# A planned attention + squared-ReLU kernel: P.V shares a ring of four PSUM banks with the layers, x of batch 1 is turned by DMA, landings are planned later

## The chip, the cores and the metric

One core of one Trainium2 chip. The metric is the device time of one execution in microseconds. Before the change three runs gave 374.03, 371.48 and 372.93 us, median 372.93 us.

## The reference

Attention with a T5 relative-position bias, followed by a feed-forward block without bias, all in fp32:

```python
# q, k, v: (8 batches, 8 heads, 576 positions, 64), bias_table: (32 buckets, 8 heads)
scores = q @ k^T / 8 + bias[bucket(|i - j|), head]      # distances >= 128 share the last bucket
attn   = exp(scores - max); attn /= sum + 1e-9
x      = (attn @ v) with heads side by side             # (4608 tokens, 512)
h      = maximum(x @ w_in, 0)                           # w_in (512, 2048)
out    = (h * h) @ w_out                                # w_out (2048, 512), out fp32
```

## The kernel before

**Attention.** The 64 (batch, head) problems are taken as 32 *pairs* of heads, four pairs to a batch (`pair(p)`). q and k of a pair arrive as fp16 in a staging buffer (`stg`, five of them) by a casting DMA of POOL's queue, and have to be turned so that the 64 head dimensions lie on partitions. In batches 0 and 1 TensorE turns them (L662) and DVE or ScalarE copies them out of PSUM; from batch 2 on (`DT_QK`) SP's queue turns them with a DMA transpose (L645). The scores are computed transposed: four runs of 128 keys by 512 queries (L707, two 64-row halves of the array, one per head), plus the last 64 keys (`last_keys`, L758) and the last 64 queries (`last_queries`, L733), which read copies spread by L689 into block-diagonal tiles `qz`. ScalarE takes the exponential of each from PSUM (L720, L768, L743), with no maximum subtracted; the far bucket's bias is taken off the table, so only a band round the diagonal has to be multiplied by `tb_sb`, the exponential of the table, on DVE (L801). Then P.V (L837 for the last keys, L844 for the rest) gives 128 queries by two heads with a column of sums, in two parts per pair (three and two query tiles). DVE takes the reciprocal of the sums (L861) and multiplies (L866) into a tile `x`.

**x turned.** Layer 1 wants x with its 512 features on partitions (`xt`, a window of three batches). For batches below `DT_X` (0 and 1) TensorE transposes 128x128 blocks into PSUM (`x_turn`, L904; four transposes for each of five query tiles) and DVE (L626) or ScalarE (L624) copies them to `xt`. From `DT_X` on SP's queue does it with a DMA transpose for each part (L882).

**Layers.** Tokens go in nine groups of 512. Layer 1 of a group is 16 tiles of four matmuls with 512 columns (L1257), ReLU on ScalarE (L1286), square on DVE (L1296). Layer 2 is done with seven products in place of eight (`second`, L1028), on sums that DVE makes of the squares (L983) and of w_out (L958); each product is 2x8 matmuls of 256 columns, and its banks are read into `y` by ScalarE (L1062) or DVE (L1056). Part of layer 1 of the last two groups is done the same way (`by_sevens`, L1182). Results leave on SP's queue (L1084).

**PSUM.** Eight banks: two double banks `st` for scores, one bank `pv` for P.V (ring `r_pv`), three banks `f` (ring `r_g`) for the turns, the layers and the tables.

**The order of the work.** [...] each engine and each queue runs its own list of instructions in order, and waits at each for the semaphores of what it needs. The lists come from a planner (`Plan`). Every piece of work is an `Op` with engines and an assumed duration, what it depends on, the buffers it holds, and a due time; `schedule()` plays a clock forward, and on each engine takes the piece that can start first, and of several the one due first. A DMA is two pieces: its issue on the queue's engine, and its flight on a resource `DMA`, which takes packets/16 ns in turn; those who need the data start after that and a latency (`LAT`). In the plan before, landings are cheap (a `DMA` duration and 1800 ns), so the consumers of a DMA stand soon behind it in their engine's list. The order that results is written down: it holds whether or not the chip is as fast as the plan assumed. Due times are formulas (`T = nominal(p)`, `G0 + GP * g`).

Of the kernel before, what the change touches and what calls it, by code (L numbers as in the profile page):

```python
# [10 lines left out]
FP32 = mybir.dt.float32  # L11
# [22 lines left out]
DT_X = 2  # L34
RELU_DVE = 0
NSTG, NQK, NPT, NV, NX, NGB, NRT, NY, NF = 5, 4, 3, 3, 6, 2, 4, 4, 2
QUIET, LATER = 5000.0, 9000
# [25 lines left out]


# [17 lines left out]
class Op:  # L82
    __slots__ = (
        "engs", "fn", "deps", "bufs", "due", "after", "mode",
        "users", "wait", "ready", "eng", "start", "end", "seq",
    )

    def __init__(self, engs, fn, deps, bufs, due, after, mode):
        self.engs, self.fn, self.bufs, self.due = engs, fn, bufs, due
        self.after, self.mode = after, mode  # L90
        self.deps = [d for d in deps if d is not None]
        self.users, self.ready = [], after
        self.start = self.end = self.eng = None
# [3 lines left out]
LAT = {"PE": 200.0, "ACT": 90.0, "DVE": 90.0, "POOL": 120.0, "DMA": 1800.0, "SP": 0.0, "XB": 2000.0}  # L97
SWITCH = 105.0


class Plan:
# [3 lines left out]
    def add(self, engs, fn, deps=(), bufs=(), due=0.0, after=0.0, mode=None):  # L105
# [3 lines left out]
        for b in op.bufs:  # L109
            b.left += 1  # L110
        return op

    def schedule(self):
# [12 lines left out]
        while len(done) < len(self.ops):  # L126
            best = None
            for e in engines:
                pick = None
                for op in waiting[e]:  # L130
# [3 lines left out]
                    key = (max(at, now[e]), op.due if op.due > -1e8 else op.ready - 1e9, op.seq)  # L134
# [15 lines left out]
            now[e] = op.end  # L150
# [9 lines left out]
            for u in op.users:  # L160
                u.wait -= 1
                if not u.wait:
                    u.ready = max(
                        [u.after]
                        + [d.end + (LAT[d.eng] if tuple(u.engs) != (d.eng,) else 0.0) for d in u.deps]
# [32 lines left out]
def kernel(  # L198
# [64 lines left out]
    pv_ps = [psum.tile([128, 512], FP32, name=f"pv{i}") for i in range(1)]  # L263
    g_ps = [psum.tile([128, 512], FP32, name=f"f{i}") for i in range(3)]

    P = Plan()
    r_set, r_pv, r_g, r_lane = Ring(2), Ring(1), Ring(3), Ring(8)
# [6 lines left out]

    def loader(eng_name, eng, out_, in_, packets, deps=(), bufs=(), due=0.0, after=0.0, turn=-1e9):
# [3 lines left out]
            {eng_name: 720.0 if eng_name == "POOL" else 600.0},  # L279
# [6 lines left out]
        return P.add({"DMA": packets / 16}, None, [issue], list(bufs) + lane, due if lane else turn), issue  # L286
# [9 lines left out]
    def load(*args, **kw):  # L296
# [8 lines left out]
            const(t[0, 0:2].rearrange("h (p j) d -> p h (j d)", j=6)), 192 * (150, 20)[w], (), [b_stg[0]], due=-5,  # L305
# [3 lines left out]
    l_id = load("SP", nc.sync, const(idsel_sb), const(id_d.ap()), 128 * 27, due=-1)  # L309
# [3 lines left out]
        128 * 27, due=0,  # L313
    )
    l_far = load("ACT", nc.scalar, const(far_sb), const(bias_table[NBK - 1 : NBK, :]), 27, due=1)
    l_oh = load("SP", nc.sync, const(oh_sb), const(oh_d.ap()), 128 * 60, due=4)
# [15 lines left out]
    z_one = P.add({"DVE": 60.0}, lambda: io(nc.vector.memset(one_sb, 1.0)), due=-2)  # L332
# [15 lines left out]
        {"DVE": 100.0},  # L348
# [8 lines left out]
    for c in range(6):  # L357
# [11 lines left out]
        o = P.add({"PE": 16 * 55.0}, t_mm, [o_eb, l_oh], [t_b], LEAD + TAB, 0.0, "f")  # L369
# [27 lines left out]
    def fill(ap, value, ns, due, after, deps=()):  # L397
        return P.add({"DVE": ns}, lambda: io(nc.vector.memset(ap, value)), deps, (), due, after)

    zz = z_sb.bitcast(FP32)  # L400
    z_fix = [[fill(zz[:, 0], 0.0, 150.0, 10, QUIET)], [fill(zz[:, 1:], 0.0, 300.0, 11, LATER)]]
    first = [
        fill(pt_sb[:, :, PW:], 1.0, 150.0, 20, LATER),
        fill(pm_sb[:, :, S:], 1.0, 150.0, 20, LATER),
# [4 lines left out]
            fill(va_sb[:, a, :, :, 64:66], VSC, 150.0, 30, at),  # L409
            *(fill(vm_sb[ds(64 * e, 64), a, :, e, 64:66], VSC, 90.0, 30, at, [o]) for e in range(2)),  # L410
        ]
        for a, ns, at in ((slice(0, 1), 250.0, QUIET), (slice(1, NV), 500.0, LATER))
# [3 lines left out]
        fill(stg[i][w][96:128, 512:640].bitcast(FP32), 0.0, 90.0, 40 + i, 25000.0)  # L416
# [25 lines left out]
    def load_six(p, w):  # L442
# [8 lines left out]
                192 * 75, (), [b_stg[p]], pdue(),  # L451
# [3 lines left out]
    def load_rows(p, w):  # L455
# [8 lines left out]
                512 * 34.5, s_fix, [b_stg[p]], pdue(),  # L464
            )
            for e in range(2)
# [5 lines left out]
                128 * 34.5, s_fix, [b_stg[p]], pdue(),  # L472
# [14 lines left out]
    def load_v_head(b, h):  # L487
# [4 lines left out]
            512 * 34.5, v_fix[min(b, 1)], [b_v[b]], pdue(),  # L492
# [3 lines left out]
    def load_v_tail(b):  # L496
        for e in range(2):
# [4 lines left out]
                256 * 34.5, v_fix[min(b, 1)], [b_v[b]], pdue(),  # L502
# [857 lines left out]
```

The softmax here doesn't subtract the row's maximum and nothing guards it: scores larger than these inputs give would overflow.

## Time and profile before

| what | value |
|---|---|
| three runs | 371.48, 372.93, 374.03 us (median 372.93) |
| the profiled execution: first to last instruction (its span, the only time it has) | 369.4 us |
| median less span | 3.5 us, outside the first and last instruction |
| TensorE (PE) busy | 353.9 us, 96% |
| DVE, ScalarE (ACT), GpSimd (POOL) busy | 277.0, 262.5, 185.4 us |
| granted TensorE clock | 1.000 |
| DMA moved | 44.26 MB in 162293 packets |

How to read it: the span is 369.4 us of the one execution that the profiler recorded. An engine is busy while it has an instruction in flight; matmuls overlap in TensorE's pipeline, so their own durations are longer than their distance. A row of a timeline gives start, length, engine, line, operation, output<-inputs, number of instructions, and in brackets the idle time before it with what ended it. DMA-issuing instructions of POOL are shown as busy on POOL; those of SP's queue are named SPq.

### The profile page before, as it was taken

The page shows a single profiled execution, that of the slowest core. Times are in us where ns is not written, and L with a number is a line of the kernel's source. Part 1 is how long each engine was busy: PE and PEld are TensorE (multiplying, and loading weights), DVE is VectorE, ACT ScalarE, POOL GpSimd, SP SyncE. Part 2 cuts the span into 40 slices and gives each one's busy share as a digit, 9 for nine tenths or more (in the row PEclk, how much of TensorE's full clock was granted, in tenths as well). Part 3 has the DMA queues.
Part 4 walks back from the last instruction along what each step waited for, and adds up shares of the span by engine and source line. Part 5 has one row for each costly group of instructions (what it writes and reads, how often), then busy time and mean ns, then how long its engine had stood idle before and what let it go on. Part 6 is the DMA issues. An engine that isn't in the chain of part 4 may idle for free.

```text
span 369.4 us, 10030 instructions
## 1 busy us (share of the span) xinstructions
PE 353.9 (96%) x3966; PEld 246.0 (67%) x3966; DVE 277.0 (75%) x618; ACT 262.5 (71%) x377; POOL 185.4 (50%) x343
## 2 busy tenths in 40 slices
PE   3978999899999999999999999999999999999996
PEld 2656455556587457877785468745876689657885
DVE  3997789957785498658965687669755987888693
ACT  4998989688575887689766887688758880586420
POOL 8897359295655676757845556777614100000000
PEclk9999999999999999999999999999999999999999
DMA  9999999795999999998999999999985112200022
GB/s 171 156 135 172 187 175 93 96 112 94 175 113 146 165 128 140 132 167 150 125 130 149 114 161 108 157 169 141 108 124 130 46 36 63 88 2 28 30 86 87
DMA packets 162293, 44.26 MB, mean 120 GB/s; under 512 B 145734, under 2 KB 162246, under 8 KB 162246
## 3 DMA queue, kind: packets, MB, share of 16 engines
q0 software_dynamic: 74208, 14.53, 52.0%
q1 hardware_dynamic: 87696, 28.80, 42.2%
q8 instruction: 31, 0.51, 0.6%
q10 hardware_dynamic: 342, 0.30, 0.3%
q14 instruction: 16, 0.13, 0.1%
HBM read 36.88 MB, written 9.44 MB: 125 GB/s over the span
## 4 chain that ended last, share of the span: by engine, by line
PE 88%; DVE 7%; ACT 2%; DMA 1%; issue 1%; ACTq 0%; DVEq 0%
PE f L1257 32%; PE f L1028 29%; PE pv L844 9%; PE st L707 8%; PE pv L837 2%; DVE pt L801 2%; PE st L758 2%; PE st L733 2%; PE st L1182 1%; DVE x L866 1%; DMA g<-in_q_dram 1%; PE f L662 1%; PE f L363 1%; ACT pm L768 1%; PE pv L1182 1%; DVE s L983 1%
## 5 line engine op out<-in xcount | busy, mean ns | idle before, releaser
L720 ACT ACTIVATE pt<-st 128x1024 f16<-128x1024 f32 x128 | 127.4, 1026 | 30.8 <-PE st L707 30.8
L1257 PE MATMUL f<-xt,w_in_sb 128*128 128x512 f16 (+4 forms) x656 | 127.8, 338 | 0.2 <-ACT xt L624 0.2
L1286 ACT ACTIVATE rt<-f 128x512 f16<-128x512 f32 x132 | 77.8, 602 | 38.4 <-PE f L1257 35.3
L1257 PEld LDWEIGHTS <-w_in_sb 128*128 128x128 f16 x656 | 57.9, 98 | 52.1 <-issue 12.2
L1296 DVE TENSOR_TENSOR g<-rt 128x512 f16<-128x512 f16 x132 | 57.6, 441 | 20.8 <-ACT rt L1286 19.8
L801 DVE TENSOR_TENSOR pt<-pt,tb_sb 128x1536 f16<-128x1536 f16 (+2 forms) x96 | 60.7, 640 | 15.6 <-ACT pt L720 15.1
L1028 PEld LDWEIGHTS <-g 128*128 128x128 f16 x576 | 54.5, 98 | 13.0 <-issue 4.7
L280 POOL DMA_DIRECT2D qs<-in_q_dram x79 | 55.4, 716 | 4.4 <-DMA w_out_sb<-in_moe_w_out_dram 2.6
L280 POOL DMA_DIRECT2D ks<-in_k_dram x79 | 55.3, 702 | 0.7 <-issue 0.6
L844 PE MATMUL pv<-va,pt 128*128 128x65 f16 x1280 | 54.7, 193 | 0.0
L844 PEld LDWEIGHTS <-pt 128*128 128x128 f16 x1280 | 50.2, 97 | 3.2 <-issue 1.4
L1056 DVE SCALAR_TENSOR_TENSOR y<-f,y 128x512 f32<-128x512 f32 (+1 forms) x47 | 31.4, 667 | 23.8 <-PE f L1028 23.6
L1028 PEld LDWEIGHTS <-s 128*128 128x128 f16 x432 | 41.2, 98 | 9.0 <-issue 2.5
L707 PE MATMUL st<-qt,kt 64*128 64x512 f16 x256 | 40.3, 385 | 0.9 <-ACT pt L743 0.4
L689 POOL COPY qz<-kt 64x64 f16<-64x64 f16 x58 | 18.5, 319 | 44.4 <-DMA kt<-ks 34.7
L689 POOL COPY qz<-qt 64x64 f16<-64x64 f16 x61 | 18.9, 310 | 35.4 <-DMA qt<-qs 27.3
L837 PE MATMUL pv<-vm,pm 128*128 128x130 f16 x160 | 35.3, 221 | 1.2 <-DVE x L866 1.0
L1028 PE MATMUL f<-w_out_sb,s 128*128 128x256 f16 x288 | 36.1, 273 | 0.0
L1028 PE MATMUL f<-wt,g 128*128 128x256 f16 x288 | 35.7, 273 | 0.0
L1028 PE MATMUL f<-w_out_sb,g 128*128 128x256 f16 x272 | 34.5, 273 | 0.7 <-ACT y L1062 0.7
L866 DVE TENSOR_TENSOR x<-pv,r 128x384 f16<-128x384 f32 x64 | 31.4, 490 | 2.0
L983 DVE TENSOR_TENSOR s<-g,s 128x1024 f16<-128x1024 f16 x36 | 25.6, 711 | 0.4
(90 smaller groups left out, 338.7 us busy)
## 6 DMA issues: line engine op xcount, KB each, us to landing
out_dram<-y SPq DMA_DIRECT2D x34, 256.0 KB, 2.4
f<-in_v_dram SPq DMA_DIRECT2D x24, 256.0 KB, 4.3
qs<-in_q_dram POOLq DMA_DIRECT2D x48, 64.0 KB, 4.4
ks<-in_k_dram POOLq DMA_DIRECT2D x48, 64.0 KB, 3.5
w_in_sb<-in_moe_w_in_dram POOLq DMA_DIRECT2D x4, 512.0 KB, 7.2
w_out_sb<-in_moe_w_out_dram POOLq DMA_DIRECT2D x4, 512.0 KB, 10.6
qs<-in_q_dram POOLq DMA_DIRECT2D x7, 144.0 KB, 4.6
ks<-in_k_dram POOLq DMA_DIRECT2D x7, 144.0 KB, 5.5
```

The source lines that it names most:

```text
L280: lambda: io(eng.dma_start(out=out_(), in_=in_())),
L689: io(eng.tensor_copy(out=dst[qb.slot][rw, rw], in_=src[qb.slot][rw, 512:576]))
L707: nc.tensor.matmul(sets_ps[st.slot][:, e, :], kt[rw, ts(jt, 128)], qt[rw, 0:512], start=True, stop=True,)
L720: nc.scalar.activation(out=p5(pts[pb.slot])[:, jt, :, 0:512], in_=sets_ps[st.slot], func=EXPF, scale=SCALE)
L801: io(nc.vector.tensor_tensor(out=a, in0=a, in1=t, op=MULT))
L837: nc.tensor.matmul(ps[:, i, :, :], pm[:, c : c + 128], vm[:, hp, :, 0:65], start=True, stop=False)
L844: nc.tensor.matmul(ps[:, i, e, :], pt[:, (2 * jt + e) * S + c : (2 * jt + e) * S + c + 128], va[:, jt, 2 * hp + e, 0:65], start=False, sto ...
L866: nc.vector.tensor_tensor(out=xs[xb.slot][:, qt0 : qt0 + nq, :].rearrange("p t (e d) -> p t e d", e=2), in0=ps[:, :, :, 0:64], in1=rs[rb.s ...
L1028: nc.tensor.matmul(home[bf.slot][:, ts(s_, HALF)], left(c, s_), right(c), start=(c == 0 and (s_ == 0 or apart) and (own or i not in before ...
L1257: nc.tensor.matmul(g_ps[bank.slot][:, a:z], w_in_sb[:, kk, ts(nt, 128)], xt_sb[:, kk, c : c + z - a], start=(kk == 0), stop=(kk == 3),)
L1286: io(nc.scalar.activation(out=rts[rb.slot], in_=g_ps[bank.slot], func=RELUF))
L1296: nc.vector.tensor_tensor(out=gs[gb1.slot][:, nt, :], in0=rts[rb.slot], in1=rts[rb.slot], op=MULT)
```

## The change

- `DT_X` goes from 2 to 1: x of batch 1 is turned by eight DMA transposes of SP's queue (L882) in place of 20 TensorE transposes (L904) and five copies.
- `pv_ps` and `g_ps` are one list of four banks, and `r_pv` is `r_g`: P.V, the turns, the tables and the layers take turns in one ring.
- The planner's figures: durations of issues, memsets and others; a landing has `SPARE` added to its DMA duration, 300 ns for the first loads and 2000 ns from batch 2 on and for DMA transposes and outputs; `over()` lets an engine's next piece start before the last has ended by the plan's clock; `AGAIN` sets what one engine waits between two of its own dependent pieces.
- `DUES`: a table that replaces the due times of some 200 pieces (by number) with others, so that the lists of all engines come out in another order.
- Memsets of constant parts may start from 1000 ns in place of 5000 and 9000, and those of the staging rows (`s_fix`) may run on POOL too (`fill_late`).
- `f1_last` keeps all layer-1 pieces of a group, not the last one made: who overwrites `xt` waits for all of them.

```diff
-DT_X = 2
+DT_X = 1
-QUIET, LATER = 5000.0, 9000
+QUIET, LATER = 1000.0, 1000.0
+DUES = """
+2:-11720 4:-7240 8:-7990 18:-18030 24:-23230 33:38700 40:-11430 56:-6380 58:-12660 60:-28280 62:-24060 64:-12660
...
+2155:-48680 2318:434840 2337:-29070
+"""
-LAT = {"PE": 200.0, "ACT": 90.0, "DVE": 90.0, "POOL": 120.0, "DMA": 1800.0, "SP": 0.0, "XB": 2000.0}
+LAT = {"PE": 200.0, "ACT": 90.0, "DVE": 90.0, "POOL": 120.0, "DMA": 1700.0, "SP": 0.0, "XB": 2000.0}
+SPARE = 300.0, 2000.0
+AGAIN = {"ACT": 30.0, "DVE": 30.0}
+def over(e, took, op):
+    if op.fn is None:
+        return op.spare
+    if e == "ACT":
+        return 123.0 if took > 400 else 60.0
+    if e == "DVE":
+        return 85.0 if took >= 240 else -10.0
+    return 40.0 if e == "POOL" else 0.0
...
+    def land(self, packets, deps, bufs, spare):
+        op = self.add({"DMA": packets[0] * packets[1] / 16 + spare}, None, deps, bufs, -1e9)
+        op.spare, op.packets = spare, packets
         return op
...
-            now[e] = op.end
+            now[e] = op.end - (over(e, took, op))
...
-    pv_ps = [psum.tile([128, 512], FP32, name=f"pv{i}") for i in range(1)]
-    g_ps = [psum.tile([128, 512], FP32, name=f"f{i}") for i in range(3)]
+    g_ps = pv_ps = [psum.tile([128, 512], FP32, name=f"f{i}") for i in range(4)]
-    r_set, r_pv, r_g, r_lane = Ring(2), Ring(1), Ring(3), Ring(8)
+    r_set, r_g, r_lane = Ring(2), Ring(4), Ring(8)
+    r_pv = r_g
...
-            {eng_name: 720.0 if eng_name == "POOL" else 600.0},
+            {eng_name: (775.0 if packets[0] >= 512 else 665.0) if eng_name == "POOL" else 500.0},
...
-        fill(stg[i][w][96:128, 512:640].bitcast(FP32), 0.0, 90.0, 40 + i, 25000.0)
+        fill_late(stg[i][w][96:128, 512:640].bitcast(FP32), 110.0, 1e5, 30000.0)
...
-                evac.append(P.add({"DMA": 1160.0}, None, [o], [qb, b_stg[p]], -1e9))
+                evac.append(P.land((640, 23.0), [o], [qb, b_stg[p]], SPARE[1]))
...
-                t = x_last[hp, part] = P.add({"DMA": 232.0 * nq}, None, [t], [xb], -1e9)
+                t = x_last[hp, part] = P.land((128 * nq, 23.0), [t], [xb], SPARE[1])
...
-        return [f1_last[old // GT]] if old >= 0 else []
+        return f1_last[old // GT] if old >= 0 else []
...
+    for x in DUES.split():
+        i, due = x.split(":")
+        P.ops[int(i)].due = float(due)
     for op in P.schedule():
```

## The prediction

> **What bounds the kernel now.** I read the page's busy shares and slices first:
>
> ```profile
> span 369.4 us, 10030 instructions
> PE 353.9 (96%) x3966; PEld 246.0 (67%) x3966; DVE 277.0 (75%) x618; ACT 262.5 (71%) x377; POOL 185.4 (50%) x343
> PE   3978999899999999999999999999999999999996
> ACT  4998989688575887689766887688758880586420
> ```
>
> TensorE is idle only in the first eight slices (74 us) and the last. Busy is not work, though. In the timeline two successive layer-2 matmuls start 0.109 us apart and layer-1 matmuls 0.216 us apart; from 75 us on nearly every start stands at that distance, plus about 0.095 us where the array goes over to 64-row score tiles or back. So behind 75 us the time is TensorE's work, and only what adds or removes matmuls, or lets TensorE run dry, can move it. What it waits for:
>
> ```profile
> PE f L662 <- ACT qs L481: 5.9, 1, 5.9
> PE f L904 <- DVE x L866: 1.3, 3, 0.6
> PE st L758 <- ACT pt L720: 1.3, 2, 0.8
> PE pv L837 <- DVE x L866: 1.0, 3, 0.5
> PE f L1028 <- ACT y L1062: 0.7, 1, 0.7
> ```
>
> 5.9 us is the start: q lands, is cast, is turned. The rest falls in two places, seen in the windows (each engine's busy time):
>
> ```profile
> core 0: us, PE busy (x) PEld busy (x) DVE busy (x) ACT busy (x) POOL busy (x), PEclk, DMA share, GB/s
> 0.00:38.80 38.80, 28.27 (x542) 20.10 (x542) 29.02 (x87) 31.58 (x44) 32.97 (x65) 1.00 1.29 160
> 38.80:62.00 23.20, 23.19 (x248) 12.26 (x247) 20.24 (x49) 21.34 (x32) 12.70 (x22) 1.00 1.31 160
> 62.00:75.00 13.00, 11.30 (x139) 7.75 (x136) 11.58 (x29) 9.14 (x13) 6.27 (x13) 1.00 0.75 84
> ```
>
> First the *ramp*: up to 38.8 us, where layer 1 begins, TensorE has little to do and ScalarE's exponentials set the pace (31.6 of the 33.8 us since its cast at 5.0). Then the *boundary* of batch 1, where layer 2 of group 0 begins and x of batch 1 is turned:
>
> ```profile
> 62.94 1.92 PE L1028 MATMUL f<-w_out_sb,g 128*128 128x256 f16 x16
> 65.55 1.91 PE L1028 MATMUL f<-w_out_sb,g 128*128 128x256 f16 x16 [0.69 <-ACT y L1062]
> 68.82 0.34 PE L904 MATMUL f<-id_sb,x 128*128 128x128 f16 x3
> 69.61 0.68 PE L904 MATMUL f<-id_sb,x 128*128 128x128 f16 x9 [0.45 <-DVE x L866]
> 70.97 0.33 PE L904 MATMUL f<-id_sb,x 128*128 128x128 f16 x3
> 71.62 0.45 PE L904 MATMUL f<-id_sb,x 128*128 128x128 f16 x5 [0.32 <-DVE x L866]
> 72.54 1.02 PE L1257 MATMUL f<-xt,w_in_sb 128*128 128x512 f16 x4 [0.24 <-ACT xt L624]
> ```
>
> Count in starts: 16 matmuls from 62.94 should end at 64.69, the next starts at 65.55 (0.86 late). A transpose takes 0.058 us (nine from 69.61 to 70.13), so 69.61 is 0.62 late and 71.62 is 0.48; the four matmuls at 71.91 need 0.22, so 72.54 is 0.41 late. Together 2.4 us.
>
> [...] 96% busy hides the distances above, which I use instead. [...] v loads of SP's queue issued between 20 and 45 us, beside the weights, took 14.6 us to land against 4.3 in the median.
>
> **The change part by part**, against the span of 369.4 us; the 3.5 us between it and the median of 372.93 are carried over.
>
> *x of batch 1.* 20 transposes x 0.057 = 1.1 us leave TensorE. Everything before them and after them is TensorE-bound or waits with them, so all of it counts: **-1.1**. Five copies (0.3 to 0.76 us each) leave ScalarE and DVE, off the path.
>
> *The boundary.* The lists of the changed program show that layer 1 of group 1 no longer follows its turn: after the last P.V of batch 1 come 11 of the 14 layer-2 blocks of group 0 (8 x 0.109 = 0.87 us each) and three score runs (0.62 each), 11.5 us. Under that cover x needs L861 and L866 (0.6), the transpose's issue (1.2) and landing (this row's median 3.7, at most 6.4): 8.2 at worst. So 0.62, 0.48 and 0.41 go. The 0.86 is product 2 waiting for product 1 to be read out of its bank, behind two exponentials (1.94 us) on ScalarE; one score run now lies between, but that run waits for the same exponentials, so I leave 0.4 of it. **-2.0**. Without that cover the turn by DMA would cost 0.6 + 1.2 + 3.7 = 5.5 us, at most those 8.2.
>
> *SP's queue.* The eight transposes are 8 x 1.2 us of issue. Ahead of the last (pair 7) stand the transposes of k of pair 10, which wait for its load; behind it v of batch 3 and the outputs. The pair 10 loads have the 3.3 us that the cover leaves at the slowest landing, 6 at the median, and what stands behind is needed a stage later: 0.
>
> *The ramp.* Up to the last scores of batch 1 (63.0 us now) both lists hold exactly the same TensorE work: 16 turns, 24 score runs, 16 small ones, 14 P.V parts, 5 turns of x, 16 layer-1 tiles. ScalarE's share is the same too: one cast more (0.84) and one table copy more (0.56), one turn copy (0.66) and one x copy (0.60) fewer, +0.1. It starts later: both casts are now on ScalarE, k first, and k was seen cast at 5.53 where q was cast at 5.01; q's load also stands behind the identity's on SP: +0.5. Against that, two of the three waits for P.V's bank (0.8) and the x wait of batch 0 (0.6) hold up later scores and so ScalarE, which idles 57.0 - 52.9 = 4.1 us between 5 and 62. I take 0.9 of it back: **-0.3**. Both sides: nothing bars ScalarE from losing nearly all its idle time (-3.0), and DVE gets 4.7 us more here (nine more w_out sums x 0.42, twelve more spreads x 0.19, ten memsets less x 0.15), which on 49.3 busy of 62 can make it the bound (+1.5). The early memsets are free: DVE idles 4.1 us before its first cast. Ten memsets that move to POOL (0.11 us each there) delay loads by 1.1 us, which land long before use.
>
> *Mode changes.* 150 against 149: +0.1.
>
> *Later stages.* Attention now ends 29 us of TensorE work sooner (the last scores at 257 of 347 us of work, from 286 of 348), so other engines are loaded less evenly. The worst stretch holds, for 10.1 us of TensorE (around the first products of group 1), six squares x 0.44, eight sums x 0.70, four bands x 0.53, two reciprocals and norms: 11.7 us of DVE, and 10.7 of ScalarE; another has 10.5 of ScalarE to 9.6. Before each both were slack, so most is absorbed: **+0.3**, between 0 and +2.5. The shared ring belongs here: the layers had three banks and have four, less the one or two that a P.V part holds until L866 has read it, about 1.5 us; either sign is possible, inside that range. That a transpose of x waits for all layer-1 pieces of an old group costs nothing: the window of three batches puts them some 80 us back.
>
> Sum: -1.1 - 2.0 - 0.3 + 0.1 + 0.3 = -3.0: span 366.4, and with 3.5 **369.9 us**.
>
> **The rivals.**
>
> *A, the sum as it stands*, 369.9 (368.3 to 371.5 for the ramp's +-1.5): chance 0.45.
>
> *B, the ramp opens.* With four banks P.V never holds up scores, and ScalarE idles 1 us of its 4.1: 3.0 less, 366.9. For it: most waits of TensorE before 40 us name L720, L768 or L866. Against: DVE's extra 4.7 us. 0.28.
>
> *C, nothing gained.* DVE becomes the ramp's bound (+1.5 in place of -0.3) and the uneven stretches cost their excess (2.5 in place of 0.3): 373.9. 0.15.
>
> *D, slower: POOL's queue can't load faster.* Between 74 and 290 us POOL is busy 134.4 us and stands still some 77, of which 55.3 in L689 waiting for q and k to be turned:
>
> ```profile
> POOL qz L689 <- DMA kt<-ks: 34.5, 16, 3.6
> POOL qz L689 <- DMA qt<-qs: 20.8, 10, 4.8
> ```
>
> Loads queue behind these. Attention's end moves up by 29 us, so POOL has 187 us for the 134.4; its loads ran some 18 us ahead of the scores. Waits up to 187 + 18 - 134 = 71 us are harmless, and at 77 as now TensorE would stand 6 us: 369.9 + 6 = 375.9, slower; it breaks even at 74 us of waits. For it: all is in order on one queue. Against: landings planned 2 us later put L689 later behind its transposes, which should shorten just these waits. 0.12.
>
> That the change isn't done is excluded: the built lists show P.V writing the `f` banks and eight more transposes.
>
> **How the numbers follow.** About 1% (3.7 us) is what a measurement of this kernel can tell from no change, so faster means under 369.2. A puts a third of its 0.45 there, B all: 0.43. D puts most of its 0.12 over 376.7 or near it with longer waits, and C little: 0.10. The rest is 0.47. The range runs from B with 0.9 to spare (366.0) to C's end (374.0); outside lie most of D and a tail of B.
>
> **What would show it.** No transposes of x on TensorE after 60 us; the boundary without waits for L866 or L624; L837 never waiting for L866; first layer-1 matmul between 38.5 and 40.5 us. It is wrong if L689 waits as long as now or TensorE shows gaps for L645's tiles, or if the last scores of batch 1 end over 2 us from 63.

## The result, and the profile after

The changed kernel takes 372.43 us (median of 20 executions, 370.67 to 375.60), the kernel before 372.01 us beside it (20 executions, 371.40 to 374.03): a ratio of 1.002, interval 1.0003 to 1.0038. Ratios and intervals, here and below, are estimated from all executions in the chip's faster state and are not quotients of the two medians. The forecast was 369.9 us. The profiled execution has a span of 369.6 us against 369.4. So nothing was gained, where 3 us were forecast, and the two traces say why: 2.2 us are lost before the boundary of batch 1, 2.0 us are gained from there to the end.

The page of the changed kernel, the busy totals and four of the slices (line numbers have moved by some 60: L904 is now L963, L1028 L1087, L1257 L1318, L866 L925, L844 L903, L707 L766, L720 L779, L733 L792, L758 L817, L689 L748):

```profile
PE 355.0 (96%) x3946; PEld 247.0 (67%) x3946; DVE 269.8 (73%) x616; ACT 259.4 (70%) x376; POOL 182.9 (49%) x341
PE   3988999999989999999999999999999999999996
POOL 8897466997999969966766681111000000000000
PEclk9996999999999999999999999999999999999999
```

The fourth digit of the granted clock is new: TensorE ran at less than full clock around 30 us. POOL is nearly full from the eighth to the fourteenth slice (65 to 129 us) and has almost nothing after the 24th (222 us). The longest waits of TensorE:

```profile
PE f L386 <- DMA far_sb<-in_bias_table_dram: 4.2, 1, 4.2
PE st L766 <- ACT pt L779: 1.8, 3, 0.8
PE st L792 <- POOL qz L748: 0.9, 1, 0.9
PE st L792 <- ACT pt L779: 0.8, 2, 0.5
```

The first is the start. Of the waits for an exponential (L766 and L792, 2.6 us) 2.2 us lie between 27 and 31 us, and are followed by the half clock, as the windows show (start:end, length, busy time of PE, PEld, DVE, ACT and POOL, then the clock):

```profile
26.00:28.00 2.00, 1.20 (x22) 0.64 (x19) 1.38 (x7) 1.84 (x3) 1.80 (x4) 1.00 1.83 188
28.00:30.00 2.00, 0.95 (x7) 0.36 (x7) 1.17 (x2) 2.00 (x3) 1.73 (x3) 0.91 1.25 198
30.00:32.00 2.00, 1.55 (x11) 0.78 (x9) 1.27 (x4) 1.82 (x4) 1.06 (x5) 0.50 1.78 179
32.00:34.00 2.00, 2.00 (x32) 2.00 (x32) 1.91 (x3) 1.36 (x2) 1.27 (x3) 0.50 1.74 185
34.00:36.00 2.00, 2.00 (x26) 1.24 (x23) 0.88 (x4) 0.00 (x0) 1.84 (x8) 0.50 1.26 207
```

TensorE is busy 2.15 us of the four from 26 to 30, and runs at half clock from 29.6 to 36.5 us. In the kernel before it is busy 3.85 of the same four, with P.V parts and turns of q between the scores:

```profile
26.00:28.00 2.00, 1.90 (x52) 1.37 (x48) 1.78 (x7) 1.51 (x3) 2.00 (x4) 1.00 1.52 92
28.00:30.00 2.00, 1.95 (x48) 1.44 (x45) 1.88 (x6) 1.69 (x3) 1.14 (x4) 1.00 0.87 116
```

The timeline of that place in the changed kernel: score runs with nothing between them, each waiting for the exponential of an earlier one, then P.V at half clock (0.65 us for eight matmuls, 0.40 elsewhere); meanwhile ScalarE stands still for 3 us.

```profile
27.93 0.39 PE L766 MATMUL st<-qt,kt 64*128 64x512 f16 x2 [0.80 <-ACT pt L779]
28.85 0.39 PE L766 MATMUL st<-qt,kt 64*128 64x512 f16 x2 [0.52 <-ACT pt L779]
...
32.44 0.65 PE L903 MATMUL f<-va,pt 128*128 128x65 f16 x8
```

```profile
36.35 1.94 ACT L779 ACTIVATE pt<-st 128x1024 f16<-128x1024 f32 x2 [2.99 <-PE st L766]
```

The boundary, in contrast, is as forecast. In TensorE's timeline layer 2 of group 0 starts at 65.11 us (62.94 before), product 2 follows with 0.2 us lost in place of 0.86, P.V and more products lie where the transposes of x were, and layer 1 of group 1 starts without a wait:

```profile
65.11 1.92 PE L1087 MATMUL f<-w_out_sb,g 128*128 128x256 f16 x16
66.96 0.60 PE L766 MATMUL st<-qt,kt 64*128 64x512 f16 x4
67.71 1.03 PE L1087 MATMUL f<-w_out_sb,g 128*128 128x256 f16 x8
...
81.68 3.62 PE L1318 MATMUL f<-xt,w_in_sb 128*128 128x512 f16 x16
```

Behind it one wait is new, 0.95 us at 110.5 us, for copies of q of pair 10 that POOL makes (L748):

```profile
110.52 0.38 PE L792 MATMUL st<-qz,kt 128*128 128x128 f16 x4 [0.95 <-POOL qz L748]
```

```profile
108.03 1.36 POOL L330 DMA_DIRECT2D ks<-in_k_dram  x2
109.38 0.63 POOL L614 CAST va<-f 128x512 f16<-128x512 f32 x1
109.93 0.72 POOL L748 COPY qz<-qt 64x64 f16<-64x64 f16 x3
```

q of that pair had been sent to be turned at 89.7 us; the copies stood behind loads and casts that fill POOL without a gap from 94.95 us on.

### The profile page after: what moved, and what is told of

Same layout as the page of the kernel before. It is cut to its first block, busy times and chain, and to the rows that moved or that the text cites. A ratio compares the mean times of both kernels' runs of the same rounds, so it can differ in the third digit from the quotient of the medians.

```text
span 369.6 us, 10020 instructions
## 1 busy us (share of the span) xinstructions
PE 355.0 (96%) x3946; PEld 247.0 (67%) x3946; DVE 269.8 (73%) x616; ACT 259.4 (70%) x376; POOL 182.9 (49%) x341
## 4 chain that ended last, share of the span: by engine, by line
PE 86%; DMA 4%; POOL 4%; ACT 3%; DVE 1%; issue 1%; ACTq 0%; SPq 0%; POOLq 0%; DVEq 0%
PE f L1318 30%; PE f L1087 28%; PE f L903 10%; PE st L766 8%; PE f L896 3%; ACT pt L779 2%; PE st L817 2%; PE st L792 2%; DMA bt_sb<-in_bias_table_dram 2%; POOL qs L330 2%; PE st L1242 1%; DMA xt<-x 1%; POOL ks L330 1%; DMA f<-in_v_dram 1%; PE f L1242 1%
## 5 line engine op out<-in xcount | busy, mean ns | idle before, releaser
L779 ACT ACTIVATE pt<-st 128x1024 f16<-128x1024 f32 x128 | 124.5, 1032 | 27.4 <-PE st L766 27.4
L1318 PE MATMUL f<-xt,w_in_sb 128*128 128x512 f16 (+4 forms) x656 | 129.4, 338 | 0.5 <-DVE xt L685 0.2
L1318 PEld LDWEIGHTS <-w_in_sb 128*128 128x128 f16 x656 | 58.3, 98 | 48.3 <-issue 10.9
L860 DVE TENSOR_TENSOR pt<-pt,tb_sb 128x1536 f16<-128x1536 f16 (+2 forms) x96 | 59.0, 626 | 15.7 <-ACT pt L779 12.6
L1087 PEld LDWEIGHTS <-g 128*128 128x128 f16 x576 | 55.0, 98 | 13.3 <-issue 4.7
L903 PE MATMUL f<-va,pt 128*128 128x65 f16 x1280 | 53.9, 195 | 0.0
L903 PEld LDWEIGHTS <-pt 128*128 128x128 f16 x1280 | 50.8, 99 | 1.5 <-DVE pt L860 0.2
L1087 PEld LDWEIGHTS <-s 128*128 128x128 f16 x432 | 41.4, 98 | 8.8 <-issue 2.5
L766 PE MATMUL st<-qt,kt 64*128 64x512 f16 x256 | 41.0, 389 | 2.0 <-ACT pt L779 1.8
L1087 PE MATMUL f<-wt,g 128*128 128x256 f16 x288 | 36.4, 273 | 0.0
L1087 PE MATMUL f<-w_out_sb,s 128*128 128x256 f16 x288 | 36.2, 273 | 0.0
L896 PE MATMUL f<-vm,pm 128*128 128x130 f16 x160 | 35.9, 224 | 0.0
L1087 PE MATMUL f<-w_out_sb,g 128*128 128x256 f16 x288 | 35.1, 273 | 0.3
L748 POOL COPY qz<-qt 64x64 f16<-64x64 f16 x56 | 17.6, 316 | 30.6 <-DMA qt<-qs 27.2
L925 DVE TENSOR_TENSOR x<-f,r 128x384 f16<-128x384 f32 (+1 forms) x64 | 30.5, 484 | 1.2 <-DVE r L920 0.2
L1042 DVE TENSOR_TENSOR s<-g,s 128x1024 f16<-128x1024 f16 x36 | 24.2, 685 | 0.1
L614 POOL CAST va<-f 128x512 f16<-128x512 f32 x24 | 16.7, 705 | 13.5 <-DMA f<-in_v_dram 13.1
```

What stands on the lines that cost most here:

```text
L766: nc.tensor.matmul(sets_ps[st.slot][:, e, :], kt[rw, ts(jt, 128)], qt[rw, 0:512], start=True, stop=True,)
L779: nc.scalar.activation(out=p5(pts[pb.slot])[:, jt, :, 0:512], in_=sets_ps[st.slot], func=EXPF, scale=SCALE)
L860: io(nc.vector.tensor_tensor(out=a, in0=a, in1=t, op=MULT))
L896: nc.tensor.matmul(ps[:, i, :, :], pm[:, c : c + 128], vm[:, hp, :, 0:65], start=True, stop=False)
L903: nc.tensor.matmul(ps[:, i, e, :], pt[:, (2 * jt + e) * S + c : (2 * jt + e) * S + c + 128], va[:, jt, 2 * hp + e, 0:65], start=False, sto ...
L925: nc.vector.tensor_tensor(out=xs[xb.slot][:, qt0 : qt0 + nq, :].rearrange("p t (e d) -> p t e d", e=2), in0=ps[:, :, :, 0:64], in1=rs[rb.s ...
```

## The experiments

The two suspects were the **clock** (order of the ramp thins TensorE, the clock falls) and the **order of the queues** (POOL, later SP). All ratios are against the kernel before, beside it on the same chip. *Fillers* are matmuls that nobody reads the result of. Span, mean clock and the last column, TensorE's longest wait from 66 to 130 us, are of the profiled execution.

| kernel | ratio (95%) | span, us | clock | longest wait, us |
|---|---|---|---|---|
| changed kernel | 1.002 (1.0003 to 1.0038) | 369.6 | 0.991 | 0.9 for qz |
| 20 fillers | 0.9994 (0.9974 to 1.0013) | 368.9 | 1.000 | 0.9 for qz |
| 20 fillers, 2 copies moved | 1.0029 (1.0010 to 1.0048) | 372.4 | 0.995 | 2.9 for qz |
| 12 fillers, 2 copies moved | 1.0002 (0.9985 to 1.0020) | 369.8 | 1.000 | 2.8 for qz |
| 12 fillers, 6 copies moved | 1.0044 (1.0023 to 1.0064) | 371.3 | 0.995 | 2.9 for xt |
| 12 fillers, loads late | 0.9997 (0.9974 to 1.0020) | 369.5 | 0.999 | 2.3 for xt |
| 12 fillers, loads late, x first | 0.9985 (0.9971 to 0.9999) | 370.0 | 0.999 | 1.9 for qz |
| 12 fillers, loads late, x and copies first | **0.9922** (0.9895 to 0.9949) | 369.0 | 1.000 | 0.8 for qz |
| the last without filler | 0.9973 (0.9951 to 0.9995) | 371.2 | 0.991 | 0.6 for qz |

**Filler in the ramp.**

```diff
+    WARM = {620: 7, 622: 4, 652: 4, 624: 3, 654: 2}   # behind five score runs, 26 to 31 us
     for op in P.schedule():
         if op.fn is not None:
             op.fn()
+        for _ in range(WARM.get(op.seq, 0)):
+            io(nc.tensor.matmul(g_ps[1][:, 0:256], id_sb, tb_sb[:, 0, 0:256], start=True, stop=True))
```

> The changed kernel with 20 more matmuls of 256 columns (0.109 us each, 2.2 us in all), put behind the score runs of pairs 2 and 3 between 27 and 31 us, where TensorE waits for exponentials; they write a PSUM bank that the next P.V part starts afresh. Theory CLOCK: TensorE was granted half its clock from 29.8 to 36.5 us because it had too little to do from 26 us on, and this made the ramp 2.2 us longer than before the change; with the gaps filled the clock stays at 1.0, the last scores of batch 1 end 2 to 3 us sooner (62 to 63 us in place of 65.1) and the kernel takes 369.5 to 370.5 us, ratio to the kernel before 0.993 to 0.996. Theory ORDER: the ramp is late because of what stands before what on ScalarE and DVE, and the clock only falls where TensorE waits anyway; then the ratio stays within 0.001 of the changed kernel's 1.002, or worsens by the 2.2 us.

Measured: 372.2 us (median of 22), 0.9994. In its profile the clock stays at 1.000 and the same P.V takes 0.41 us again; from its timeline:

```profile
32.06 0.41 PE L903 MATMUL f<-va,pt 128*128 128x65 f16 x8
...
63.70 1.92 PE L1087 MATMUL f<-w_out_sb,g 128*128 128x256 f16 x16
```

Layer 2 of group 0 starts at 63.70 us, 1.4 sooner than in the changed kernel and 0.8 later than before: in this pair of profiles 1.4 of the ramp's 2.2 us are the clock, shown by work that computes nothing. Over all profiles of kernels with this ramp the start has a median of 64.18 us with filler (eight, 63.62 to 65.58) and 65.11 us without (seven, 64.52 to 66.67), so 0.9 us is the safer figure. The mean clock is under 0.997 in 4 of 22 executions, against 17 of 20 of the changed kernel and 8 of 27 of the kernel before: in that one, too, the clock falls at times. The time that theory CLOCK forecast (0.993 to 0.996) did not come: what goes on behind the ramp took part of the gain back, 1.4 us there, 0.7 in the span, and the interval overlaps that of the changed kernel.

**Each part alone**, on the kernel before: `DT_X = 1`, then the one ring of four banks.

```diff
-DT_X = 2
+DT_X = 1
```

> The kernel before with x of batch 1 turned by DMA alone, all else as before. The step of the prediction: 1.1 us of transposes leave TensorE for certain. The waits of the boundary (1.5 us of them at transposes and the copy) go only if something covers the DMA's 5.5 us; the old due times put layer 1 of group 1 three blocks behind the last P.V, so a wait for x of up to 3 us may take their place. If the gain is in the turn itself: 0.993 to 0.997. If it needs the new order: 0.998 to 1.004.

```diff
-    g_ps = [psum.tile([128, 512], FP32, name=f"f{i}") for i in range(3)]
+    g_ps = pv_ps = [psum.tile([128, 512], FP32, name=f"f{i}") for i in range(4)]
...
-    r_set, r_pv, r_g, r_lane = Ring(2), Ring(1), Ring(3), Ring(8)
+    r_set, r_g, r_lane = Ring(2), Ring(4), Ring(8)
+    r_pv = r_g
```

> The kernel before with P.V in one ring of four banks with the layers, all else as before. If P.V's single bank cost the ramp its 0.8 us of waits for the normalisation: 0.996 to 0.999, without a wait of P.V for it. If ScalarE sets the ramp anyway: 0.999 to 1.002. A clock below 1.0 in the ramp here would say that the ring, not the new due times, thins TensorE out.

Measured: 376.34 us, 1.0099 (1.0069 to 1.0129), and 377.89 us, 1.0152 (1.0123 to 1.0182), both above all that was expected. Both lose in the ramp: layer 2 of group 0 starts at 66.31 and 67.05 us (62.94 before), and in both the clock falls there. From that start to the end they need 2.0 and 3.3 us more than the kernel before, so the turn alone gains nothing there: the gain at the boundary needs more of the change. With the ring alone no P.V waits for L866 any more, as meant, but L707 and L758 wait 4.7 us for exponentials in place of 2.5. Three windows of the run with the turn alone, the thin one ahead of the fall:

```profile
24.00:26.00 2.00, 1.26 (x16) 0.66 (x17) 1.90 (x13) 2.00 (x3) 1.55 (x6) 1.00 2.11 137
26.00:28.00 2.00, 1.52 (x32) 1.38 (x30) 1.97 (x5) 1.42 (x3) 2.00 (x4) 0.71 1.12 70
28.00:30.00 2.00, 2.00 (x29) 1.04 (x30) 1.11 (x5) 1.38 (x2) 1.34 (x3) 0.50 1.19 73
```

So the fall of the clock belongs to neither of these parts; each of these new orders of the ramp ran into it. The planner's figures and the early memsets were not tried alone.

**The table of due times**: all of it left out, then kept from piece 945 on.

```diff
-DUES = """
-2:-11720 4:-7240 8:-7990 ...
+DUES = """
 """
```

> The changed kernel without its table of due times: the formulas order all lists, with the new planner's figures, the ring and the DMA turn. If the table is what thins TensorE out in the ramp (theory CLOCK or ORDER both allow it), the granted clock stays at 1.0 throughout and the last scores of batch 1 end at 62 to 63.5 us; the table's other work is lost, so the boundary can wait for x as in the turn alone: 0.995 to 1.005. If the clock falls here too, the table is not the cause.

```diff
     for x in DUES.split():
         i, due = x.split(":")
-        P.ops[int(i)].due = float(due)
+        if int(i) >= 945:
+            P.ops[int(i)].due = float(due)
```

> The changed kernel with its table of due times from piece 945 on only: loads and batches 0 and 1 go by the formulas. Theory CLOCK (the table's order of the ramp thins TensorE and so costs 1.4 us): the ramp ends up to 1.4 us sooner with the formulas. Rival ORDER (any order of the ramp under four banks and late landings thins TensorE; the table is the better one): the clock is below 1.000 here too, the ramp ends later than 65.1 us, and the time lies between the changed kernel's 372.4 and the 380.1 of the kernel without any table.

Measured: 380.08 us, 1.0194 (1.0160 to 1.0228), with a mean clock of 0.982 to 0.991; and 385.0 us, 1.0349 (1.0326 to 1.0372), 0.982 to 0.996; neither time lies where it was expected. The table doesn't cause the fall of the clock, which comes without it too, and is worth 1.7% in this kernel. Used from piece 945 on only, it was worse than none.

**Copies ahead of loads on POOL.** First the two copies of q of pair 10 (alone, with 20 fillers, with 12):

```diff
+    early = [o for o in order if o.seq in (1013, 1014)]      # spread copies of q of pair 10
+    order = [o for o in order if o.seq not in (1013, 1014)]
+    at = [o.seq for o in order].index(296)                   # k load of pair 18
+    order[at:at] = early
```

> The changed kernel with one move on POOL: the two spread copies of q of pair 10 stand ahead of the seven loads and v casts that kept them from 95 to 109.9 us. Theory POOL (its in-order queue holds TensorE up at 110 us): the 0.95 us gap before L792 is gone; span 369.6 - 0.9 = 368.7, ratio to the changed kernel 0.9975, so about 0.9995 of the kernel before. Rival LOADS (the seven loads that now stand 0.5 us later are themselves late): the gap comes back a few us on as a wait for a load or a transpose, ratio 1.002 as for the changed kernel.

> The 20 filler matmuls between 26 and 34 us and the moved spreads of pair 10 together. If clock and POOL's queue are separate losses they add: 1.002 - 0.0026 - 0.0025 = 0.997 of the kernel before, 370.9 us. If POOL's queue paces the stretch up to 125 us, what the filler gains in the ramp waits there anyway: 0.9995, as either alone.

> As the run with both, with 12 filler matmuls in place of 20 (4, 2, 2, 2, 2 behind the same five score runs). If the filler only has to keep TensorE from being idle more than half of the time, 12 (1.3 us of work) hold the clock as 20 do, and the ramp ends 0.3 us sooner, since less filler lies on TensorE's path: 0.996. If 20 were needed, the clock falls to half between 30 and 36 us as without filler (mean 0.991 to 0.995) and the time is that of the moved spreads alone, 0.9995.

Measured: 374.39 us, 1.0051 (1.0034 to 1.0068); 373.19 us, 1.0029; 371.93 us, 1.0002. The expectation failed: the wait for pair 10 went, and the second copy of q of pair 12, four pieces further on in POOL's list, became the late one, by more:

```profile
PE st L792 <- POOL qz L748: 2.8, 1, 2.8
```

That line is from the run with 12 fillers, in which POOL ends that copy at 111.93 us (it starts at 111.69) and the score run starts at 111.98. Twelve fillers hold the clock as 20 do (2 of 22 executions under 0.997).

Then all six late copies, q and k of pairs 10, 12 and 13 (with 12 fillers, and without):

```diff
...
+    MOVE = {1013: 236, 1014: 236, 1163: 236, 1195: 296, 1196: 296, 1197: 296}   # piece: ahead of which load
...
```

> The run with 12 filler matmuls, and on POOL all six late spread copies moved: q of pairs 10 and 12 directly behind the first copy of q of pair 12, q and k of pair 13 ahead of the last three k loads of pair 18. Theory QUEUE (the data had landed by 102 us; the copies only stand behind loads and casts in POOL's order, and with two of them moved the next one, q of pair 12, was the late one): no wait of TensorE for L748 any more, against 0.9 us in the changed kernel and 2.8 us with 12 fillers and two copies moved; span 369.8 - 2.8 = 367.0, or 368.0 if 1 us comes back as a wait for x of batch 2 at 121 us; ratio 0.993 to 0.996 of the kernel before. Rival LANDING (the transposes land late, whatever the order): the wait stays between 1 and 3 us and the ratio at 1.000.

> The same six copies moved on POOL, without filler. QUEUE: the 0.95 us before 110.5 us go, and in the executions in which this wait is longer, more; ratio 0.998 to 0.999 of the kernel before in place of 1.002, the clock still half for 3 to 7 us of the ramp in most executions. LANDING: 1.002 to 1.005.

Measured: 374.6 us, 1.0044, and 377.04 us, 1.0109 (1.0069 to 1.0149), both above all that was expected. No wait for qz is left, and one for x of batch 2, on its way through SP's queue, takes its place:

```profile
PE f L1318 <- DMA xt<-x: 2.9, 1, 2.9
```

How one queue hands it to the other is to be seen in this run: SP's load of v waits for the buffer that POOL's cast frees, the cast had been pushed back by the copies (it starts at 107.48 us in the changed kernel), and SP starts 0.03 us after it.

```profile
108.67 0.60 POOL L614 CAST va<-f 128x512 f16<-128x512 f32 x1
```

```profile
109.30 0.37 SPq L330 DMA_DIRECT2D f<-in_v_dram  x1
```

The wait has a second price: in this run the clock falls behind it (0.83 in the window from 120 to 130 us), and the mean clock is under 0.997 in 13 of 19 executions in spite of the filler.

```profile
120.00:130.00 10.00, 8.23 (x53) 4.38 (x53) 2.96 (x9) 4.28 (x8) 8.82 (x18) 0.83 1.37 169
```

**Loads out of the way.** Five loads of pair 18, which is turned at 135 us only, go behind the v cast of 114 us; the six copies go ahead of the v cast of 107 us (`move` puts the pieces of its first argument ahead of its second).

```diff
...
+    move((290, 292, 296, 298, 300), 302)
+    move((1013, 1014, 1163, 1195, 1196, 1197), 319)
```

> The changed kernel with the 12 filler matmuls, and on POOL five loads of pair 18 (3.6 us of issue, not needed before 135 us) put behind the v cast at 114 us, with the six spread copies of pairs 10, 12 and 13 ahead of the v cast that SP's next v load waits for. Theory QUEUE (the stretch from 90 to 125 us is paced by what POOL has to do in order; moving copies alone only handed the wait on, over the v cast and SP's v load to the x transposes of batch 2): with work taken out of that stretch both waits go: no wait for L748 over 0.3 us, none for xt over 0.5; against 2.8 and 0 with 12 fillers and two copies moved, and 0 and 2.9 with six moved: span 367.0 to 367.5, ratio 0.993 to 0.996. Rival XT (SP's own list of transposes paces layer 1 of group 2, POOL or not): the wait for xt is 1 to 3 us again, ratio 0.999 to 1.004.

> The same without filler. QUEUE: ratio 0.996 to 0.999 of the kernel before, with TensorE's clock at half for 3 to 7 us of the ramp in most executions. XT: 1.002 to 1.008, with 1 to 3 us of wait for xt.

Measured: 371.78 us, 0.9997, and 373.55 us, 1.0037. The rival was right: the wait for xt stays (2.3 and 2.1 us). SP's own list explains it. With filler, DVE has x of pair 10 ready at 112.69 us, but SP first issues the transposes of q of pair 15, x of pair 11 and k of pair 15, and x of pair 10 (the fourth, with 2.47 us of issue) lands just before 121.56, when layer 1 goes on:

```profile
112.13 0.56 DVE L925 TENSOR_TENSOR x<-f,r 128x384 f16<-128x384 f32 x1
```

```profile
111.69 1.24 SPq L704 DMA_TRANSPOSE qt<-qs  x1
113.02 1.22 SPq L941 DMA_TRANSPOSE xt<-x  x1
114.42 1.20 SPq L704 DMA_TRANSPOSE kt<-ks  x1
115.71 2.47 SPq L941 DMA_TRANSPOSE xt<-x  x1
```

**x first on SP.** Two kernels moved the transposes of x of pairs 10 and 11 up in the list, ahead of those of pair 15. They turn x of pair 10 before it is normalised, so layer 1 reads other data there, and their times (374.53 and 373.92 us) answer nothing.

> The run with 12 fillers, late loads of pair 18 and early spread copies, and on SP's queue the transposes of x of pairs 11 and 10 put ahead of those of q and k of pair 15. Theory SP (with POOL relieved, the order of SP's list decides when layer 1 of group 2 can start): x of pair 10 is issued 2.6 us sooner and lands near 119 us, and the 2.3 us before L1318 at 121.6 us fall under 0.5; span 369.5 - 2.0 = 367.5, ratio 0.9945 of the kernel before (0.992 to 0.997). Rival DMA (landings, not issues, are late: the transpose takes 5.8 us whenever it is issued, behind other packets): the wait stays over 1.5 us or comes back as a wait for q or k of pair 15 within 10 us, ratio 0.999 to 1.002.

> The same without filler: the wait for xt near 122 us (2.1 us in the run before it) falls under 0.5 by theory SP; ratio 0.998 (0.996 to 1.000) in place of 1.0037, what is left being the ramp's half clock. Rival DMA: 1.003.

Two others get the same order on SP by putting q and k of pair 15 behind x of pair 10:

```diff
...
+    at = [o.seq for o in order].index(1034) + 1                          # transpose of x of pair 10
+    order[at:at] = [o for o in order if o.seq in (1254, 1256)]           # of q and k of pair 15
+    del order[[o.seq for o in order].index(1254)]
+    del order[[o.seq for o in order].index(1256)]
```

> The run with 12 fillers, late loads of pair 18 and early spread copies, and on SP's queue the transposes of q and k of pair 15 put behind those of x of pairs 11 and 10. Theory SP: x of pair 10, made at 112.7 us, is issued at 113 in place of 115.7 and lands near 119; the 2.3 us before L1318 at 121.6 us fall under 0.5; span 369.5 - 2.0 = 367.5, ratio 0.9945 of the kernel before (0.992 to 0.997). Rival DMA (landings, not issues, are late): the wait stays over 1.5 us, or comes back as a wait for q or k of pair 15 within 10 us, ratio 0.998 to 1.002.

> The same without filler: by theory SP the wait for xt near 122 us (2.1 us in the run before it) falls under 0.5; ratio 0.998 (0.996 to 1.000) in place of 1.0037, what is left being the ramp's half clock. Rival DMA: 1.003.

Measured: 371.14 us, 0.9985, and 373.45 us, 1.0038. The wait for xt is gone, as theory SP said, but the times are those of its rival, because the next copy in POOL's list, k of pair 14, is late:

```profile
123.08 0.42 PE L817 MATMUL st<-qt,qz 128*128 128x288 f16 x2 [1.87 <-POOL qz L748]
```

**And the next copies.**

```diff
...
+    move((1228, 1229), 308)                   # copies of k of pair 14, ahead of k loads of pair 19
+    move((1258, 1259, 1260, 1261), 332)       # copies of pair 15, ahead of the loads of pair 20
```

> The run before it with filler (x of pair 10 ahead of q and k of pair 15 on SP), and on POOL the spread copies of k of pair 14 ahead of two k loads of pair 19, those of pair 15 ahead of six loads of pair 20. Theory ORDER OF THE QUEUES: the 1.9 us before L817 at 123.1 us go and nothing takes their place: TensorE waits less than 0.5 us in all between 66 and 130 us, span 370.0 - 1.9 = 368.1, ratio 0.994 (0.992 to 0.997). Rival TOO MUCH WORK on the queues: a wait of 1 to 2 us for another copy, transpose or v load appears before 135 us, ratio 0.998 to 1.000.

> The orders of POOL's and SP's queues of the run before it, without filler matmuls. If the two losses are separate and add: 0.9922 x 1.002 / 0.9994 = 0.995 (0.993 to 0.998), no wait over 1 us between 66 and 130 us, clock half for 3 to 7 us of the ramp in most executions. If the ramp's lateness moves the queues' waits about, so that the orders fit only the warm ramp: 1.000 to 1.004 and a wait over 1 us again between 66 and 130 us.

Measured: 369.4 us, 0.9922 (0.9895 to 0.9949, 6 executions), all at full clock; without filler 371.61 us, 0.9973 (22 executions). TensorE's waits from 66 to 130 us with filler are now these two, both before 88 us:

```profile
PE st L817 <- POOL qz L748: 0.8, 1, 0.8
PE f L1318 <- DMA xt<-x: 0.5, 1, 0.5
```

This is a version that beats the kernel before, by 2.5 us in the median (371.91 beside it). It nearly completes a square: neither 1.002; filler (20) 0.9994; orders of the queues 0.9973; both (12 fillers) 0.9922. Clock and queues are two losses, 1.0 and 1.7 us alone and 3.6 us together, and within their intervals they add. The square is not quite even: 12 fillers alone were not run, and on the same queues 12 gave about 1.0 us more than 20 (1.0002 and 1.0029), as much as the two losses lack. In all seven pairs that compute the same and differ in the filler alone, the filler gains, 0.8 to 1.0 us with 20 matmuls (two pairs) and 1.5 to 2.4 us with 12 (five); the two kernels that read other data, left out here, go the other way.

## Why the prediction was wrong

**x of batch 1 (-1.1) and the boundary (-2.0): right.** No transpose of x on TensorE after 60 us (L963 has 20, the last at 40.8 us), no wait for L925 at the boundary. From the start of layer 2 of group 0 to the end the changed kernel needs 304.5 us against 306.5; adding the 0.95 and 0.24 us of new waits at 110 and 121 us the gain is 3.2, where 3.1 was forecast for these two terms. Of the 3.2 us between the forecast span (366.4) and the measured one, 2.5 lie in the ramp and 0.7 behind it. With both losses out the ratio of 0.9922 on 372.0 us gives 369.1.

**The ramp (-0.3): this step failed.** It measured +2.2. I took it for certain that TensorE has time to spare there and costed only ScalarE and DVE, and so asked whether the same work would find the same engines, not whether TensorE would be busy enough. ScalarE was to win back 0.9 us of idle time and lost 3.2: it idles 8.6 us between 5 and 65.1 us, against 5.4 between 5 and 62 before. (The 4.1 of the forecast is a slip: the 52.9 us of busy time include a table load of 1.28 us that ends before 5.)

The traces show two states of the clock (1.00 and 0.50) and falls of two lengths. In the 20 profiles of this case the clock falls 18 times, 13 times for 3.4 us and 5 times for 6.8, the changed kernel's 29.6 to 36.5 among them; and where it falls more than once in a profile, the later falls lie 4, 7, 19, 20 or 28 times 3.41 us behind the first. The run with six copies moved and no filler has one of each length; its clock changes at 29.58, 36.41, 125.15 and 128.57 us, as the shares in these windows say:

```profile
29.50:29.60 0.10, 0.00 (x0) 0.00 (x0) 0.10 (x1) 0.10 (x2) 0.10 (x2) 0.90 1.16 195
36.40:36.50 0.10, 0.10 (x7) 0.10 (x6) 0.10 (x1) 0.10 (x1) 0.10 (x2) 0.96 1.23 205
125.10:125.20 0.10, 0.10 (x2) 0.00 (x0) 0.00 (x0) 0.00 (x0) 0.10 (x2) 0.77 2.40 154
128.50:128.60 0.10, 0.10 (x3) 0.09 (x1) 0.00 (x0) 0.00 (x0) 0.10 (x1) 0.67 2.15 165
```

Of the 175 executions of the changed kernel and its variants with a mean clock under 0.997, 155 lose 0.004 to 0.006 or 0.009 to 0.011 of it; half of 3.4 or 6.8 us in 370 is 0.005 or 0.009. In the 3.41 us ahead of a fall TensorE was not idle but busy, for 1.70 us in the changed kernel and for 0.37 to 1.96 us in all 18. No threshold follows, because four stretches of that length in mid-kernel, at whole multiples of 3.41 us from a fall, with 1.58 to 1.75 us of busy time passed at full clock. Nor does the longest wait decide: the changed kernel's clock fell with none over 0.8 us between 5 us and the fall; with one of 2.8 us (12 fillers, 2 copies moved) the mean clock was 1.000, with one of 2.9 us (20 fillers, 2 copies moved) 0.995. How a thin stretch lies to those multiples may decide it, and may be why executions of one kernel differ in their clock; that is my estimate from these figures, not shown.

Half clock made 0.9 to 1.4 of the 2.2 us; the rest, at full clock, is the later start with both casts on ScalarE (q is cast at 5.77 us in place of 5.01) and other waits for exponentials, which the runs don't separate. DVE (the +1.5 of the range) was not the bound there: ScalarE's 2.99 us were a wait for TensorE. That 372.4 us lies within the stated range, towards rival C, is luck: of C's two costs, DVE as the bound and the uneven stretches, neither was found.

**SP's queue (0) failed, and so did the place of "later stages" (+0.3).** I placed the risk in DVE and ScalarE in uneven stretches. In the changed kernel no wait of TensorE for DVE appears after 66 us; 0.9 to 3.8 us of waits for POOL's copies or SP's transposes do, in the changed kernel and its variants. For SP I counted issue time and slack for the eight transposes alone, and not what will stand ahead of the next batch's. In the changed kernel's own profile SP's queue costs 0.24 us (x at 121 us); its 1.1 to 3.8 us came where POOL's copies had been moved away.

**Rival D had the right queue, the opposite order and the wrong measure.** It feared loads that come late behind copies that wait; what came late were copies behind loads. It set the sum of POOL's waits (77 us) against the sum of its slack from 74 us to the end of attention, and found 71 us to be harmless. The waits did shrink, as argued: those of the copies for turned q and k from 55.3 to 30.5 us, though 6.5 us came back in which loads wait for the same transposes. But slack at 240 us can't be spent at 110. The windows of the kernel before:

```profile
62.00:90.00 28.00, 26.30 (x243) 16.49 (x240) 21.75 (x47) 21.45 (x32) 18.71 (x36) 1.00 0.86 96
90.00:125.00 35.00, 35.00 (x398) 24.74 (x399) 24.48 (x54) 23.45 (x32) 20.38 (x38) 1.00 1.37 146
```

and of the changed kernel:

```profile
62.00:90.00 28.00, 27.85 (x309) 19.79 (x307) 19.71 (x42) 18.46 (x25) 25.20 (x46) 1.00 1.56 173
90.00:125.00 35.00, 33.66 (x388) 23.05 (x385) 24.73 (x55) 26.23 (x38) 34.02 (x64) 1.00 1.60 171
```

POOL (the fifth busy time) goes from 20.38 to 34.02 of 35 us: loads for 20 us and more ahead and copies for now, in one list. TensorE (the first) loses 1.3 there. The stretch has enough time for the work, as the last pair of runs shows; it was the order. In this kernel q and k are cast on POOL's queue and turned on SP's; no run here tries it otherwise.

**Other claims.** P.V never waits for the normalisation: right. Mode changes (+0.1): nothing in the trace speaks against it; in the rows above L766 starts at 66.96 us, 0.10 behind 65.11 + 16 x 0.109. First layer-1 matmul between 38.5 and 40.5 us: wrong, 41.76; last scores of batch 1 more than 2 us from 63: so it was (65.11), and that was named as the sign of a wrong forecast. The 3.5 us between span and median are not all outside the first and last instruction, as the table of the kernel before has it: 1.8 lie there in the executions of both kernels, and the rest was that the profiled one was quicker than the median of three; against the later median of 372.0 the sum should have carried 2.6, which makes the forecast 369.0.

What stays open: executions of the changed kernel at the same mean clock differ by up to 4 us (371.34 to 375.60 at 0.991). Waits at 110 to 122 us between 0.9 and 3.8 us in the profiles of its variants are of that size, but no profile of a long execution of the changed kernel itself was taken.

## What to carry to other kernels

Before a stage is reordered, ask how busy TensorE is in each 2 to 4 us of it. Where it fell to about half or less in these runs (0.37 to 1.96 of the 3.41 us ahead of a fall), the price was not only the wait but, often, half the clock for 3.4 or 6.8 us, and a dozen empty matmuls (12 x 0.109 = 1.3 us, by my estimate mostly hidden in the waits) were the better bargain. Count an in-order queue's slack stretch by stretch, never as a sum, and follow what stands ahead of each small piece that TensorE needs now: loads for later belong behind it. When one wait has been removed and another as long appears on the neighbouring queue, suspect the order of both; here only the last move showed a clear gain.

## What the runs showed of the hardware

- Half clock in the middle of a kernel, in 17 of 20 executions of the changed one, with no wait of TensorE longer than 0.8 us between 5 us and its fall in the profile, and for 3.4 or 6.8 us in every profile that shows it. Twelve matmuls of 256 columns kept it off in 20 of 22 executions (2 copies moved) and in all 28 of the last two kernels with filler, but in only 8 of 14 and 6 of 19 where a wait of 2.3 or 2.9 us at 120 us followed.
- A DMA transpose of x on SP's queue takes 1.2 us of issue in the median of the changed kernel and up to 2.77 us; with loads late SP issued almost without a break from 107 to 124 us.
- Three copies of 64x64 in a row on POOL took 0.72 us in the changed kernel and 1.51 and 2.26 us in the two kernels with loads late (with 12 fillers and without). What lengthened them was not shown.
